# Moving a decay factor from the output of eight retention jobs into the turn of their q

## The chip, the cores and the metric

The kernel runs on one core of a Trainium2 chip. Its time is the device time of one execution in microseconds (us). Before the change three runs took 1150.2, 1152.78 and 1153.15 us, median 1152.78.

## The reference

Retention attention over q, k, v of shape (8 batches, 8 heads, 576 positions, 64), float32, is followed by a gated feed-forward block on 4608 tokens of width 512 (inner width 1536):

```python
gamma = 1.0 - 2.0 ** (-5.0 - np.arange(H))
Dmat  = np.where(rel >= 0, gamma[:, None, None] ** rel, 0.0)      # rel = i - j
attn  = ((q @ k.T) / np.sqrt(64) * Dmat) @ v                      # by batch and head
x     = attn.transpose(0, 2, 1, 3).reshape(4608, 512)
xn    = x / np.sqrt(mean(x * x) + 1e-6) * rms_g
out   = (silu(xn @ w_gate) * (xn @ w_val)) @ w_out
```

The three weight matrices come as 64-bit floats and are rounded to 32 bits in the kernel.

## The kernel before

A *job* is one batch and one pair of heads: 32 jobs, whose tiles hold two heads of 64 on 128 partitions. A *unit* is 384 tokens of the feed-forward block: 12 units. The instructions of each engine stand in the order in which the Python code writes them (a manual schedule), and each engine works through its own list in order.

A job works in chunks of L = 64 positions, nine in all. The decay gamma^(i-j) is split into a factor of the row and one of the column. Column factors gv scale v (`scale_v`, L255, ScalarE). Row factors, gamma^(i+L)/8 in the table gq, are applied to the result: `carried` (L362) multiplies it by gq when it copies it from PSUM into x (L390, VectorE). In between `scores` (L272) multiplies q and k within a chunk, `states` (L292) multiplies k and v, `weigh` (L305, VectorE) masks the scores, `sums` (L319, VectorE) adds up the states over chunks, `values` (L344) multiplies masked scores and v, and the products in `carried` add q times the summed states. A memset of one element, `tick`, on GpSimd (L359) stands between values and carried products.

`slot(j)` (L397) does values of job j-1, scores, states, masking and sums of job j, and the carried products of job j-1. The first eight jobs (j < 2*NHP, two batches) are loaded as they lie in memory by `load_first` (L145), and `turn(j)` (L216) turns their q and k on TensorE: for q, eight matrix products of a slice of q with the identity `ident` (L230); for k, four transposes (L224); for the last 64 rows, the tails, two transposes (L238). ScalarE copies the results into qT and kT (L235, L244). Later jobs are turned by VectorE in `prepare`, and use the tables gq and gx in `carried`.

`start()` (L846) writes out the beginning. Small tables are sent by `table(i, queue)`, chunk 0 of the weights by ScalarE's queue, the loads of the eight jobs by SP's queue. Then, for each of eight jobs: `slot(j)`, `turn(j + 1)`, adding up of squares, `scale_v`, the square of x of the job before (L432, ScalarE), steps of the weights' rounding (VectorE at L752 to L797, three Relu on ScalarE at L768), and for unit 0 `norm_1`, `diagonals` and `norm_2`. From L905 on the products of units 0 and 1 (`up_plain`, L564) follow, with the rounding of the other chunks beside them. Rows 8 and up of `w_up`, the tiles w_gate and w_val, hold data on its way at that time; columns 256 and up of rows 0 to 7 are not written until the second group of weight chunks.

Units 2 to 11 use seven block products instead of eight (`up` at L507, `across` at L629), with the later jobs in between. GpSimd makes the sums of weight blocks for that in `combine` (L811).

Of the kernel before, what the change touches and what calls it, by code (L numbers as in the profile page):

```python
# [22 lines left out]
def _decay_tables(H, D):  # L23

    pairs = _gamma(H).reshape(H // 2, 2).T
    rows = np.repeat(pairs, D, axis=0)
    pos = np.arange(L)
    p = np.concatenate([pos, pos])  # L30
    gq = rows[:, :, None] ** (pos + L) / np.sqrt(D)
    t = pairs.T[None] ** -p[:, None, None], rows**L, gq, np.roll(gq, D, axis=0)
    return [np.ascontiguousarray(x).astype(np.float32) for x in t]


# [6 lines left out]
def kernel(  # L42
# [64 lines left out]
    gx = const.tile([P, NHP, L], F32, name="gx")  # L107
    gv = const.tile([P, NHP, 2], F32, name="gv")
    gc = const.tile([P, NHP], F32, name="gc")
    tick = const.tile([1, 1], F32, name="tick")  # L110
    rms_g = const.tile([P, NHP], F32, name="rms_g")
    w_out = const.tile([P, NF, DM], F32, name="w_out")
# [87 lines left out]
    def load_kv(j):  # L200
# [12 lines left out]
            out=t, in_=v[b, 2 * hp : 2 * hp + 2, NFULL * P :].rearrange("e p d -> p e d")  # L213
        )

    def turn(j):  # L216

        d = st[j]
        last = bank(f"turn_{j}_t")
        for nm in "qk":  # L220
            ps = bank(f"turn_{j}_{nm}")
            for c in range(NFULL):
                if nm == "k":
                    nc.tensor.transpose(  # L224
                        out=ps[:, c * P : c * P + P],
                        in_=d["k"][:, c].rearrange("p e d -> p (e d)"), identity=ident,
                    )
                    continue
                for e in range(2):
                    nc.tensor.matmul(  # L230
                        ps[side(e), c::NFULL], lhsT=d["q"][:, e, c], rhs=ident,
                        start=True, stop=True,
                    )
            t = d[nm + "T"] = att.tile([P, S], F32, tag=nm + "T", name=f"{nm}T_{j}")
            nc.scalar.copy(out=t[:, : NFULL * P], in_=ps)  # L235
        for i, nm in enumerate("qk"):
            o = slice(i * TAIL, i * TAIL + TAIL)
            nc.tensor.transpose(  # L238
                out=last[:, o], in_=d[nm + "t"].rearrange("p e d -> p (e d)"),
                identity=ident[:TAIL, :TAIL],  # L240
            )
        for i, nm in enumerate("qk"):
            o = slice(i * TAIL, i * TAIL + TAIL)
            nc.scalar.copy(out=d[nm + "T"][:, NFULL * P :], in_=last[:, o])  # L244
# [117 lines left out]
    def carried(j):  # L362

        d = st[j]
        b, hp = jobs[j]
        av = d["av"]
        for c in range(1, NC):
            i, odd = divmod(c, 2)
            for e in range(2):
                mm = nc.tensor.matmul(  # L370
                    av[odd][column(j, odd, e), i * L : i * L + L], lhsT=d["sum"][side(e), c - 1],
                    rhs=d["qT"][side(e), c * L : c * L + L],
                    start=False, stop=(c >= NC - 2), skip_group_check=True,
                )
                if c == 1 and e == 0:
                    follow(mm, d["valued"])
        for c0, c1 in ((0, 2 * HU), (2 * HU, S)) if b % 2 == 0 else ((0, HU), (HU, S)):
            u, o = divmod(b * S + c0, U)
            if u not in x_of:
                x_of[u] = xp.tile([P, NHP, U], F32, tag="x", name=f"x_{u}")  # L380
            x = x_of[u][:, hp, o : o + c1 - c0].rearrange("p (c k) -> p c k", k=L)
            for first in (c0 // L, c0 // L + 1):
                i, odd = divmod(first, 2)
                n = -(-(c1 // L - first) // 2)
                moves = [(slice(0, P),) * 2]
                if column(j, odd, 0) != side(0):
                    moves = [(side(e), column(j, odd, e)) for e in range(2)]
                for to, at in moves:
                    g = (gq if to == at else gx)[at, hp].unsqueeze(1)
                    nc.vector.tensor_tensor(  # L390
                        out=x[to, first - c0 // L :: 2],
                        in0=av[odd][at, i * L : (i + n) * L].rearrange("p (c k) -> p c k", k=L),
                        in1=g.to_broadcast([at.stop - at.start, n, L]), op=ALU.mult,
                    )
        st[j] = {}
# [450 lines left out]
    def start():  # L846

        h_of[0] = ffn.tile([P, NF, U], F32, tag="h", name="h_0")
        tables = list(zip((causal, gv, gc, gq, gx), (_causal_table(), *_decay_tables(H, D))))

        def table(i, queue):
            t, values_ = tables[i]
            src = nc.inline_tensor(values_, name=t.tensor.name + "_table")
            queue.dma_start(out=t, in_=src.ap())

        make_identity(nc, ident)
        nc.scalar.activation(out=tick, in_=mhalf[:1], func=AF.Silu)
        nc.vector.memset(ones, 1.0)
        warm = bank("warm")
        for _ in range(6):  # L860
            nc.tensor.matmul(warm[:, :P], lhsT=ones, rhs=ones, start=True, stop=True)
        first_places.update(find_places())
        load_chunks(1)
        for i in (1, 0, 2):
            table(i, nc.scalar)
        weights(3)
        for j in range(2 * NHP):
            load_first(j, {0: range(2), 1: range(2, H), NHP: range(H)}.get(j))
            if j == 1:
                table(3, nc.sync)  # L870
            load_chunks((1, 1, 1, 1, 2, 2, 2, 3)[j], nc.sync)
        table(4, nc.sync)
        nc.sync.dma_start(out=rms_g, in_=moe_rms_g.rearrange("(c p) -> p c", p=P))
        load_chunks(4, nc.sync)
        turn(0)
        scale_v(0)
        act(3)
        squares = []
        for j in range(2 * NHP):
            slot(j)  # L880
            if j + 1 < 2 * NHP:
                turn(j + 1)
            if squares:
                gather(*squares.pop())
            for i in ((1,), (2,), (3,), (4, 5), (6,), (7,), (), ())[j]:
                scale_v(i)
            if j:
                u, c = divmod(j - 1, NHP)
                squares.append((u, c, square(u, c)))
            act(1)  # L890
            if j == 5:
                norm_1(0)
            elif j == 6:
                norm_2(0)
            weights((2, 0, 0, 1, 1, 1, 1, 0)[j])
            if j == 4:
                gather(*squares.pop())
            elif j == 5:
                diagonals(0)
            act(1)  # L900
        gather(*squares.pop())
        load_qk(2 * NHP)
        load_kv(2 * NHP)
        made = combine_out()
        for m, g in [(m, g) for g in range(NG) for m in range(2)]:  # L905
            for u in range(2):
                weights_to(4 * g + 2 * m + 1)
                for i, _ in enumerate(up_plain(u, m, g)):
                    if not (u or m or g):
                        if i == 0:  # L910
                            values(2 * NHP - 1)
                            carried(2 * NHP - 1)
                            gather(1, NHP - 1, square(1, NHP - 1))
                        elif i == 1:
                            norm_1(1)
                        elif i == 2:
                            diagonals(1)
                        elif i == 3:
                            norm_2(1)
                    weights(2)  # L920
                    act(1)
                    if u and m and g == NG - 1:
                        weights_to(len(chunks))
                        next(made, None)
                    if i == 1:
                        weights_to(4 * g + 2 * m + 2)
        for _ in made:
            pass
        for blk, t in first_blocks.items():
            keep(blk, t)  # L930
        rest = across(1)
        next(rest)
        following(2 * NHP - 1)
        for i, _ in enumerate(rest):
            if i == 1:
                norm_0(2)
            elif i == 3:
                norm_1(2)
                diagonals(2)
        rest = across(0)  # L940
        next(rest)
        combine(1)
        slot(8, rest=False)
        following(8)
        for i, _ in enumerate(rest):
            if i == 2:
                norm_2(2)
        combine(0)
        slot(9)
        following(9)  # L950
# [71 lines left out]
```

## Time and profile before

| | |
|---|---|
| median of three runs | 1152.78 us |
| the profiled execution | 1153.15 us, span 1151.4 us |
| TensorE (PE) busy | 1126.5 us, 98% of the span |
| VectorE (DVE) busy | 716.0 us, 62% |
| ScalarE (ACT) busy | 244.0 us, 21% |
| GpSimd (POOL) busy | 50.8 us, 4% |
| chain that ended last | PE 90%, DVE 3%, DMA 2% |

The profile is one execution. In its rows a line such as L390 is a line of the kernel before; a row of the timeline has the start in us from the span's start, the time in us, the engine, the line, the operation, the tile written and the tile read, the shape, the number of instructions merged, and in brackets the engine's idle time before it with what ended it. "ACTq" and "SPq" are the queues' own instructions, DMA issues among them. "issue" is time in which an engine waited for nothing that the profile shows. The granted clock is TensorE's, 1.00 being full speed.

### The profile page before, as it was taken

Reading aid. Unit: us, or ns where it says so; the run is one execution under the profiler, and the core shown is the slowest. Engines: PE = TensorE matmul, PEld = TensorE weight load, DVE = VectorE, ACT = ScalarE, POOL = GpSimd, SP = SyncE. Lnnn points to the kernel's source line nnn. Section 1 sums busy time; section 2 is a strip of 40 time slices with the busy share of each in tenths; the row PEclk is TensorE's granted clock in tenths of the full one; section 3 lists DMA queues with packets and bytes.
Section 4 is the critical chain, followed back from the end, with each engine's and each line's share of the span. In section 5 each row is a group of like instructions: output and inputs, shape, how many; then the busy total and the mean of one; then the engine's idle time right before and its main releaser. Section 6 shows DMA issues by size and latency. Waiting matters only on the chain.

```text
span 1151.4 us, 24802 instructions
## 1 busy us (share of the span) xinstructions
PE 1126.5 (98%) x10524; PEld 1053.4 (91%) x10524; DVE 716.0 (62%) x1420; ACT 244.0 (21%) x480; POOL 50.8 (4%) x74
## 2 busy tenths in 40 slices
PE   8799999989999999999999999999999999999998
PEld 6655557989999999999999999999999999999998
DVE  5788858675675675365766675465576566445352
ACT  5546542002201211211221120120220220120210
POOL 0000000570000000000000000000000000000000
PEclk8999999999999999999999999999999999999999
DMA  8764336335453565044345456306436503403304
GB/s 203 207 184 147 109 131 193 56 59 117 115 130 67 146 141 160 1 105 102 97 119 73 116 144 119 114 29 120 117 80 140 144 19 93 128 1 99 122 1 110
DMA packets 292943, 125.42 MB, mean 109 GB/s; under 512 B 270432, under 2 KB 275808, under 8 KB 292832
## 3 DMA queue, kind: packets, MB, share of 16 engines
q1 hardware_dynamic: 282688, 107.66, 38.1%
q10 hardware_dynamic: 10144, 16.16, 4.3%
q8 instruction: 83, 1.36, 0.5%
q14 instruction: 28, 0.23, 0.1%
HBM read 108.83 MB, written 14.94 MB: 108 GB/s over the span
## 4 chain that ended last, share of the span: by engine, by line
PE 90%; DVE 3%; DMA 2%; POOL 1%; ACT 1%; issue 1%; SPq 0%; DVEq 0%; POOLq 0%; ACTq 0%
PE x L507 14%; PE w L507 14%; PE z L507 13%; PE up L564 8%; PE xo L629 8%; PE wo L629 7%; PE zo L629 7%; PE y L507 7%; PE yo L629 4%; PE av L351 2%; PE av L370 2%; PE s L280 2%; POOL w_gate L811 1%; PE s L300 1%; DMA w_gate<-in_moe_w_out_dram 1%
## 5 line engine op out<-in xcount | busy, mean ns | idle before, releaser
L531 ACT COPY m<-x 128x384 f32<-128x384 f32 x60 | 28.8, 479 | 449.8 <-PE x L507 425.5
L629 PE MATMUL xo<-h,w_out 128*128 128x192 f32 x528 | 90.3, 328 | 0.0
L507 PE MATMUL w<-sums,w_val 128*128 128x192 f32 x480 | 88.6, 328 | 0.6 <-DVE c L514 0.3
L507 PE MATMUL x<-x,w_gate 128*128 128x192 f32 x480 | 89.0, 329 | 0.0
L507 PE MATMUL x<-x,w_val 128*128 128x192 f32 x480 | 88.8, 328 | 0.0
L507 PE MATMUL z<-x,w_gate 128*128 128x192 f32 x480 | 87.8, 326 | 0.0
L507 PE MATMUL w<-sums,w_gate 128*128 128x192 f32 x480 | 87.8, 326 | 0.0
L507 PE MATMUL z<-x,w_val 128*128 128x192 f32 x480 | 87.8, 326 | 0.0
L629 PEld LDWEIGHTS xo<-h,w_out 128*128 128x128 f32 x528 | 85.9, 190 | 0.6
L629 PE MATMUL wo<-h,w_out 128*128 128x192 f32 x504 | 85.3, 326 | 0.0
L629 PEld LDWEIGHTS wo<-h,w_out 128*128 128x128 f32 x504 | 82.5, 190 | 0.0
L514 DVE TENSOR_TENSOR u<-m,y 128x384 f32<-128x384 f32 x60 | 33.1, 552 | 79.2 <-PE y L507 79.1
L507 PEld LDWEIGHTS w<-sums,w_val 128*128 128x128 f32 x480 | 79.2, 190 | 2.9 <-DVE c L514 2.9
L507 PEld LDWEIGHTS x<-x,w_gate 128*128 128x128 f32 x480 | 79.6, 191 | 0.5
L507 PEld LDWEIGHTS z<-x,w_gate 128*128 128x128 f32 x480 | 79.8, 190 | 0.0
L507 PEld LDWEIGHTS x<-x,w_val 128*128 128x128 f32 x480 | 79.1, 190 | 0.6
L507 PEld LDWEIGHTS z<-x,w_val 128*128 128x128 f32 x480 | 79.6, 190 | 0.0
L507 PEld LDWEIGHTS w<-sums,w_gate 128*128 128x128 f32 x480 | 79.6, 190 | 0.0
L514 DVE TENSOR_TENSOR h<-u,w 128x384 f32<-128x384 f32 x60 | 33.0, 551 | 71.0 <-PE w L507 71.0
L526 ACT ACTIVATE h<-h 128x384 f32<-128x384 f32 x90 | 47.1, 523 | 88.6 <-DVE h L514 88.6
L564 PE MATMUL up<-x,w_gate 128*128 128x384 f32 x192 | 63.3, 488 | 0.9 <-DVE x L476 0.7
L564 PE MATMUL up<-x,w_val 128*128 128x384 f32 x192 | 62.7, 487 | 0.2 <-ACT w_val L572 0.2
(170 smaller groups left out, 1769.8 us busy)
## 6 DMA issues: line engine op xcount, KB each, us to landing
w_out<-w_blocks SPq DMA_DIRECT2D x70, 768.0 KB, 5.1
out_dram<-o SPq DMA_DIRECT2D x368, 24.0 KB, 1.6
qraw<-in_q_dram SPq DMA_DIRECT2D x96, 72.0 KB, 2.7
kraw<-in_k_dram SPq DMA_DIRECT2D x96, 72.0 KB, 2.8
k<-in_k_dram SPq DMA_DIRECT2D x48, 128.0 KB, 3.0
v<-in_v_dram SPq DMA_DIRECT2D x48, 128.0 KB, 2.9
w_out<-in_moe_w_gate_dram ACTq DMA_DIRECT2D x5, 1024.0 KB, 5.8
w_out<-in_moe_w_out_dram ACTq DMA_DIRECT2D x3, 1024.0 KB, 4.9
```

Of the source, the lines that this page charges most:

```text
L280: nc.tensor.matmul(s[side(odd), e, i * L : i * L + L], lhsT=d["kT"][side(e), c * L : c * L + L], rhs=d["qT"][side(e), c * L : c * L + L], ...
L300: nc.tensor.matmul(o[side(e)], lhsT=d["k"][side(odd), i, e], rhs=d["v"][side(odd), i, e], start=True, stop=True,)
L351: mm = nc.tensor.matmul(av[odd][column(j, odd, e), i * L : i * L + L], lhsT=d["v"][side(odd), i, e] if c < NC - 1 else d["vt"][:, e], rhs= ...
L370: mm = nc.tensor.matmul(av[odd][column(j, odd, e), i * L : i * L + L], lhsT=d["sum"][side(e), c - 1], rhs=d["qT"][side(e), c * L : c * L + L],
L507: nc.tensor.matmul(ps[:, i * HU : i * HU + HU], lhsT=w_up[m][:, 2 * blk + c, cut], rhs=t_of[u][blk][:, c], start=(start and i == c == 0), ...
L514: nc.vector.tensor_tensor(out=o, in0=a, in1=pairs_of(ps), op=ALU.add)
L526: nc.scalar.activation(out=o, in_=c, func=AF.Silu)
L531: nc.scalar.copy(out=s1, in_=pairs_of(x_))
L564: nc.tensor.matmul(ps[:, :U], lhsT=w_up[m][:, 4 * half + c, i * P : i * P + P], rhs=x_of[u][:, c], start=(c == 0), stop=(c == NHP - 1),)
L629: nc.tensor.matmul(ps[:, i * HU : i * HU + HU], lhsT=a[:, c, i * P : i * P + P], rhs=rhs[:, c], start=(start and i == c == 0), stop=False, ...
L811: nc.gpsimd.tensor_tensor(out=o, in0=a, in1=b, op=op)
```

## The change

The row factor gamma^(i+L)/8 of the first eight jobs goes into q when it is turned, instead of into the result. The right side of the products in `turn` is no longer the identity but a diagonal matrix of factors: by head, four of 128 x 128 and one of 64 x 64 for the tail. They lie in columns of w_gate and w_val that are free at that time. Eight heads have the same factors in both batches, so they are made once, as products of the identity and a new table `turned` (128 x 40): for job 0 on VectorE, for jobs 1 to 3 on GpSimd. The tail of q becomes two products instead of half of the transposes. x is then a plain copy from PSUM, made by ScalarE in place of VectorE's product. The table `turned` is sent first on ScalarE's queue, ahead of chunk 0; the table gq, now needed by job 8 first, is sent after the loads of the eight jobs instead of after job 1's.

The words that came with the change also name the norm of the third unit; the diff has no line on it.

```diff
@@ _decay_tables
+    at = np.stack([(4 * np.arange(P) + i) % L for i in range(4)] + [np.arange(P) % L], axis=1)
+    t += (_gamma(H)[None, :, None] ** (at[:, None, :] + L) / np.sqrt(D),)
@@ new functions
+    def factors(j, e):
+        h = 2 * jobs[j][1] + e
+        main = w_up[0][:, h, 2 * P : 6 * P].rearrange("p (i t) -> p i t", t=P)
+        return main, w_up[1][:TAIL, h, 4 * P : 4 * P + TAIL]
+
+    def make_factors(j, engine):
+        for e in range(2):
+            main, tail = factors(j, e)
+            g = turned[:, 2 * jobs[j][1] + e]
+            engine.tensor_tensor(
+                out=main, in0=ident.unsqueeze(1).to_broadcast([P, NFULL, P]),
+                in1=g[:, :NFULL].unsqueeze(2).to_broadcast([P, NFULL, P]), op=ALU.mult,
+            )
+            engine.tensor_tensor(
+                out=tail, in0=ident[:TAIL, :TAIL],
+                in1=g[:TAIL, NFULL:].to_broadcast([TAIL, TAIL]), op=ALU.mult,
+            )
@@ turn
-                        ps[side(e), c::NFULL], lhsT=d["q"][:, e, c], rhs=ident,
+                        ps[side(e), c::NFULL], lhsT=d["q"][:, e, c], rhs=factors(j, e)[0][:, c],
...
-        for i, nm in enumerate("qk"):
-            o = slice(i * TAIL, i * TAIL + TAIL)
-            nc.tensor.transpose(
-                out=last[:, o], in_=d[nm + "t"].rearrange("p e d -> p (e d)"),
-                identity=ident[:TAIL, :TAIL],
-            )
+        for e in range(2):
+            nc.tensor.matmul(
+                last[side(e), :TAIL], lhsT=d["qt"][:, e], rhs=factors(j, e)[1],
+                start=True, stop=True,
+            )
+        nc.tensor.transpose(
+            out=last[:, TAIL : 2 * TAIL], in_=d["kt"].rearrange("p e d -> p (e d)"),
+            identity=ident[:TAIL, :TAIL],
+        )
@@ carried
                 for to, at in moves:
+                    if j < 2 * NHP:
+                        nc.scalar.copy(
+                            out=x[to, first - c0 // L :: 2],
+                            in_=av[odd][at, i * L : (i + n) * L].rearrange("p (c k) -> p c k", k=L),
+                        )
+                        continue
                     g = (gq if to == at else gx)[at, hp].unsqueeze(1)
@@ start
+        table(5, nc.scalar)
         load_chunks(1)
         for i in (1, 0, 2):
             table(i, nc.scalar)
+        for j in range(NHP):
+            make_factors(j, nc.gpsimd if j else nc.vector)
         weights(3)
         for j in range(2 * NHP):
             load_first(j, {0: range(2), 1: range(2, H), NHP: range(H)}.get(j))
-            if j == 1:
-                table(3, nc.sync)
             load_chunks((1, 1, 1, 1, 2, 2, 2, 3)[j], nc.sync)
+        table(3, nc.sync)
         table(4, nc.sync)
```

More of the change, by code (lines that the diff above doesn't have):

```diff
@@ L109 @@
     gc = const.tile([P, NHP], F32, name="gc")
+    turned = const.tile([P, H, NFULL + 1], F32, name="turned")
     tick = const.tile([1, 1], F32, name="tick")
@@ L848, in start @@
         h_of[0] = ffn.tile([P, NF, U], F32, tag="h", name="h_0")
-        tables = list(zip((causal, gv, gc, gq, gx), (_causal_table(), *_decay_tables(H, D))))
+        tables = list(zip((causal, gv, gc, gq, gx, turned), (_causal_table(), *_decay_tables(H, D))))
         def table(i, queue):
```

## The prediction

> **What bounds the kernel now.** I began with TensorE's time by stage, since the edits lie in the first eight jobs. Columns: stage, its length, busy time of PE, PEld, DVE, ACT, POOL, granted clock, DMA share, GB/s.
>
> ```profile
> 0.00:75.00 75.00, 61.59 (x1356) 48.97 (x1356) 52.10 (x153) 37.98 (x87) 4.85 (x16) 0.93 0.80 200
> 75.00:180.00 105.00, 104.70 (x324) 61.55 (x325) 82.32 (x95) 59.40 (x70) 0.00 (x0) 1.00 0.38 128
> 10.00:20.00 10.00, 9.76 (x252) 8.54 (x253) 7.21 (x19) 7.38 (x17) 0.09 (x1) 0.74 0.96 217
> ```
>
> From 75 us on TensorE has no idle time that the change could reach (104.70 of 105.00). So the change is worth what it moves the products of the two first units, at 68.34 and 75.09 us. Next the timeline of the first job: what holds ScalarE and the clock there.
>
> ```profile
> 3.75 0.36 ACTq L854 DMA_DIRECT2D gv<-gv_table  x1
> 4.05 1.56 PE L230 MATMUL turn_q<-ident,h 128*64 128x128 f32 x16
> 6.63 0.69 DVE L752 TENSOR_SCALAR w_gate<-w_out 128x1024 uint32<-128x1024 uint32 x1 [5.50 <-DMA w_out<-in_moe_w_gate_dram]
> 7.90 0.33 ACTq L854 DMA_DIRECT2D causal<-causal_table  x1
> 8.02 0.69 PE L224 MATMUL turn_k<-ident,first_k 128*128 128x128 f32 x4 [2.41 <-DMA first_k<-in_k_dram]
> 8.76 0.59 ACT L235 COPY qT<-turn_q 128x512 f32<-128x512 f32 x1 [6.54 <-DMA gv<-gv_table]
> 9.93 0.54 ACT L260 ACTIVATE first_sums<-first_sums,gv 128x256 f32<-128x256 f32 x1
> ```
>
> ScalarE's queue issues gv, causal and gc, and its first copy comes after the last of them (8.28 + 0.44). From 9.93 to 15.25 ScalarE is the chain: four scalings, three Relu of 1.15, the next copies. Then the timelines of slots 6 and 7, for VectorE, and of the rounds of weights on GpSimd, for what two engines cost each other.
>
> ```profile
> 48.48 0.94 DVE L390 TENSOR_TENSOR x<-av,gq 128x128 f32<-128x128 f32 x4
> 56.11 2.19 DVE L476 SCALAR_TENSOR_TENSOR x<-x,rms_g,rb 128x384 f32<-128x384 f32 x4
> 62.36 0.28 DVE L329 SCALAR_TENSOR_TENSOR sum<-sum,gc,last 128x64 f32<-128x64 f32 x1
> 62.56 0.94 DVE L390 TENSOR_TENSOR x<-av,gq 128x128 f32<-128x128 f32 x4
> ```
>
> ```profile
> 210.06 1.32 DVE L641 TENSOR_TENSOR w_val<-w_val 128x1152 f32<-128x1152 f32 x1
> 218.62 2.35 DVE L641 TENSOR_TENSOR t<-h 128x1152 f32<-128x1152 f32 x1
> L811 POOL TENSOR_TENSOR w_val<-w_val x12: 1269/1274/2385, 215.8 to 233.6; 128x512 f32<-128x512 f32 x12
> ```
>
> The same subtraction took 1.32 us with GpSimd idle and 2.35 with GpSimd at work, and GpSimd's own 1.27 grew to 2.39 at worst.
>
> **The change, part by part** (times of the profiled execution, line numbers of before).
>
> *x on ScalarE.* VectorE loses 8 x 0.94 = 7.5 us. ScalarE gains four copies a job. A 512-column copy starts 0.58 after the one before it, a 64-column one 0.11, so 1.05 ns a column and 0.04 each; columns 192, 192, 128, 64 make 0.24 + 0.24 + 0.17 + 0.11 = 0.76 us a job. They stand ahead of the qT copy, which waits for turn_q anyway: 16 records, 1.09 us. That hides them; without it they cost 0.76 x 7 = 5.3. If they don't overlap (0.22 for 64 columns alone, so 1.22 together) 0.13 shows in each of seven slots, 0.9 in all. In slots 2 and 3 the second scaling of v ends last (27.72 + 0.51, the products of L300 at 28.35), so VectorE's relief is worth nothing there. In the slot of turn 6 the copies stand behind the Relu that ends at 46.98, so qT 6 starts near 47.75 instead of 46.89; but the six products of ms (48.09 to 48.85) come first on TensorE, and values start near 48.95 instead of 48.85. Price 0.1, ends 0 and 0.86.
>
> *VectorE's relief.* It lies between 45 and 66 us, where VectorE is nearly full. Without x at 48.48, r (49.35) can follow ms, which ends at 48.92, and GpSimd's power and the diagonals come 0.4 earlier. L476 starts when rb ends, and rb, by the waits in the built order, no longer waits for ScalarE's kT (55.16, idle 0.24 before). So the sums of job 7, which end at 62.64, end some 0.3 earlier if TensorE's pause of 1.01 at 49.65 (put down to "issue") remains, and 0.4 + 1.0 = 1.4 earlier if it goes. TensorE waited 0.55 for these sums. After them x of jobs 6 and 7 leaves VectorE, but the square of job 7 now waits for all four copies instead of two, 0.15 later. I take -0.8, the middle, ends -1.4 and -0.3.
>
> *Start.* The table turned goes out first on ScalarE's queue, so chunk 0 is issued about 0.45 later (0.43 an issue). The built order shows that DMAs share eight semaphores in turn, so each waits for the one eight before it. With one more in front, gv waits for k (7.90) where it waited for q (3.75), causal for chunk 0, gc for the tail of k. Causal, issued at 7.90, took 2.5 to land; gv then lands near 10.4 to 10.5, and the scalings that start at 9.93 wait: 0.5 us, with the Relu and the next job's copies queued behind. Ends 0.35 (the issue alone) and 1.1 (gc's 3.1 landing).
>
> Job 0's factors are four VectorE products, two of 512 columns at 0.69 (0.55 for 384 in L438, plus 128 x 1.04 ns) and two of 64 at about 0.2: 1.8 us. No row has the table's landing; q's 3.0 and gv's 5.0 bound it, I take q's, the issue nearest in time: 3.8. But GpSimd's twelve products are released by the same landing: six of 1.35 (three took 3.97 in a row) and six of about 0.25, 9.6 us. By the row of L641 a product loses about 1.0 to the other engine. The second half's factor, needed by turn_q's second product, then ends at 7.0 (VectorE first) or 8.35 (GpSimd first). turn_q takes 1.09, or 1.97 at half clock as at 12.20, turn_k 0.66 or 1.12. So turn_k ends between 8.8 and 11.4 instead of 8.71. In the first case ScalarE's copies set the scores (9.1 + 0.5 + 0.6 = 10.2), in the second turn_k does (11.4 + 0.6 + 0.1): 0.3 to 2.3 after 9.89. Rounding of chunk 0 (0.69, 0.69, 1.23) shifts from 6.63 to about 8.8, with a wait for GpSimd each, to 13.1 us; the masked scores began at 12.29. The two delays overlap. I take +1.2, ends +0.5 and +2.3: nearer to the low end, since the Relu from 11.2 covers part. GpSimd ends its list near 17.9 (3.8 + 9.6 + 4.4 of VectorE's turns); the first tick memset, which waited until 16.39, is queued behind it, and carried products (17.6 now, 18.8 then) wait for that tick.
>
> [...]
>
> *gq's table moved.* It passes the loads of jobs 2 to 7 on SP: 0.61 of issue and 128 KB less ahead of them. Only job 5's v was waited for (1.86 + 0.26), in a stretch where TensorE paused 2.33 for its own reasons. I take -0.2, ends -0.6 and 0. It then stands before gx, rms_g and one chunk, whose loads win as much before: nothing.
>
> *Turns of q, tails.* Same products with another right side. A tail is two products and a transpose: five records for two, some 0.02 us each (40 of L280 in 0.76), 0.5 in all, within the 0.24 us that values waited after each turn. Nothing, ends -0.3 and +0.5. TensorE's five pauses under "issue" (0.35, 1.07, 2.33, 1.01, 0.81) come at heavy DMA; the change hardly alters that. Nothing, ends -2 and +2.
>
> *The third unit's norm.* The change's words name it, no line of the diff touches it, and the built order has it in one place in both: nothing.
>
> **Sum.** +1.2 - 0.2 + 0.1 - 0.8 = +0.3 us. The ends without the pauses: 0.5 - 0.6 + 0 - 1.4 - 0.3 = -1.8 and 2.3 + 0 + 0.9 - 0.3 + 0.5 + 0.9 = +4.3. The profiled execution was 1153.15 us, of which the span is 1151.4; the median of the runs is 1152.78. On the median: 1153.1.
>
> **Rivals.** No difference beyond 0.3% (3.5 us, about what a measurement of this kernel can tell from no change) is the forecast: a late start given back by VectorE. 0.65.
>
> *Slower, by GpSimd's list.* Place: first tick and the factors of job 0. If the table lands like gv, after 5.0 us (at 5.9), GpSimd ends near 20.0 and VectorE's factor near 10.4; turn_q at half clock ends at 12.4, turn_k at 13.5, and after a copy of 0.6 the scores start near 14.2, 4.3 later than 9.89. It decides once the second factor is later than k's landing (7.9) by more than the 0.8 that the relief gives back. +4.3 - 0.8 + 0.1 = +3.6, 1156.4 us; more with copies that don't overlap. [...] Against: q landed in 3.0. 0.20.
>
> *Faster, by the relief.* The pause at 49.65 moves off the chain and relief is 1.4 us; the 2.33 pause at 35.87 and the half clock after it (turn_q 1.98 for 1.09, turn_k 1.12 for 0.66) go, because job 5's loads are earlier: 0.5 - 1.4 - 2.33 - 1.35 = -4.6, of which ScalarE's chain behind job 5's v (its last scaling starts at 37.97) gives back about 0.8. -3.8, 1149.0 us. For it: TensorE waited for sums of job 7. Against: the DMA queue stays full (share 1.04 in 30 to 40). 0.15.
>
> *ScalarE becomes the bound* lies inside the forecast: +0.9 at most.
>
> **Range.** From the faster case, 1149.0, to the slower one with the copies in part exposed, 1157.0; beyond either lies some 1 in 10.
>
> **What would show it.** Right: gv issued near 8 us, scores of job 0 starting between 10.2 and 12.2, L390's place taken by ScalarE copies of 0.76 to 1.22 us a job, values of job 7 before 62.56 plus the delay at the start, and TensorE without idle time after 75 us. Wrong: GpSimd's factors over 1.9 us each, a first tick that carried products wait for by over 1 us, copies of x that turn_q doesn't hide, or pauses under "issue" that differ by more than 2 us in all.

## The result, and the profile after

The changed kernel took 1158.82 us (median of four runs, 1157.52 to 1159.65) against 1152.61 us for the kernel before on the same chip: 6.2 us more, ratio 1.0057 with a 95% interval of 1.004 to 1.0074. Its profiled execution was 1159.65 us, span 1157.8. The kernel became slower, by 0.6%.

The stages first, in the columns of the prediction, and as a fourth one the later part that the prediction had called full.

```profile
0.00:75.00 75.00, 63.25 (x1372) 51.45 (x1373) 51.36 (x122) 42.10 (x117) 15.69 (x28) 0.93 0.80 200
75.00:180.00 105.00, 104.13 (x323) 60.90 (x322) 81.81 (x95) 57.86 (x66) 0.00 (x0) 1.00 0.39 129
10.00:20.00 10.00, 7.94 (x194) 6.67 (x198) 9.39 (x16) 7.49 (x18) 5.03 (x7) 1.00 0.92 208
620.00:960.00 340.00, 333.58 (x3478) 328.07 (x3477) 208.77 (x450) 57.91 (x130) 3.62 (x15) 1.00 0.40 98
```

The same late stretch of the kernel before:

```profile
620.00:960.00 340.00, 339.53 (x3515) 333.61 (x3515) 213.78 (x460) 58.82 (x131) 3.62 (x15) 1.00 0.42 100
```

Between 620 and 960 us, where no line of the diff is at work, TensorE is busy 333.58 us of 340 instead of 339.53. That is 5.95 us, about the whole loss. The waits of TensorE from 75 us on say what it waited for. Columns: waiting tile and line, what it waited for, us in total, times, longest.

```profile
PE av L397 <- issue: 4.6, 3, 1.7
PE av L397 <- POOL tick L386: 3.4, 2, 3.1
PE x L540 <- issue: 1.5, 1, 1.5
```

Before there was one such pause under "issue" after 75 us, 0.9 us long; now four make 6.1 us. One of them in the timeline of TensorE:

```profile
649.84 0.22 PE L397 MATMUL av<-qT,sum 64*64 64x64 f32 x1
649.85 0.22 PE L327 MATMUL s<-v,k 64*64 64x64 f32 x1
649.85 0.62 PE L397 MATMUL av<-qT,sum 64*64 64x64 f32 x24
652.06 0.34 PE L397 MATMUL av<-qT,sum 64*64 64x64 f32 x7 [1.59 <-issue]
```

Carried products stop in the middle of a row of equal products, and the profile shows no input that they wait for. I counted TensorE's records up to each such pause of 0.3 us or more: weight loads, products and its sequencer's own instructions, nearly all of them waits for semaphores (165 in the kernel before, 175 after the change), in order of start. In the kernel before they stand at records 706, 1218, 1475, 1986, 2498 and 5570; after the change at 1218, 1730, 12738, 13250, 16322 and 18114. Divided by 256 all of these leave 194 or 195; counted without the sequencer's, the remainders drift (184 at the first pause before, 152 at the last). So the pauses stand at fixed places in the instruction stream, a whole number of 256 records apart; a *block* below is 256 records from one such place on. The DMA table has a queue of kind "instruction" with 83 packets of 16 KB, and the records, 21213 before and 21271 after the change, are 82.9 and 83.1 blocks:

```profile
q8 instruction: 83, 1.36, 0.5%
```

With 256 records more, in the run with 64 products below, it has 84. So I read a packet as one block. In the 14 profiles of this study there are 69 such pauses after 12 us, and not one stands elsewhere. TensorE went on 1.23 to 1.71 us after the end of the block's packet; at none of the 1151 block starts that I could match did it go on earlier than 1.22 us behind a packet. The packet itself takes about 1 us (0.88 to 1.73 before and after the change). In the pauses it starts after TensorE has entered the block before: 1.15 to 4.3 us after in the first 75 us, where loads are dense (DMA share 0.80), and 0.5 to 3.6 us after later on. In the long products 256 records take some 20 us (20.3 is the median of all blocks before), and no late block follows such a stretch. In a slot, with its products of 64 x 64, a block is gone sooner: those ahead of the late ones took 2.1 to 4.0 us without the pause, and 2.75 to 6.0 us in the first 75 us.

The change adds 48 weight loads and products (10548 of each instead of 10524). A tail that was two transposes (two loads, two products) is now two matrix products and one transpose, and each of these matrix products leaves two loads and two products:

```profile
51.91 0.33 PE L261 MATMUL turn_t<-w_val 64*64 64x64 f32 x4
52.17 0.27 PE L265 MATMUL turn_t<-ident,w_val 64*128 64x64 f32 x1
```

That is six more a job, for eight jobs. With them come ten more waits of the sequencer, so that from slot 8 on every block begins some 58 records earlier in the work, and other work stands at the block starts. The expectations below count the 48 alone.

The start, as the timeline has it:

```profile
4.14 1.55 POOL L231 TENSOR_TENSOR w_gate<-ident,turned 128x512 f32<-128x512 f32 x1 [2.84 <-DMA turned<-turned_table]
5.69 0.68 DVE L231 TENSOR_TENSOR w_gate<-ident,turned 128x512 f32<-128x512 f32 x1
6.30 5.30 DVE L235 TENSOR_TENSOR w_val<-ident,turned 64x64 f32<-64x64 f32 x1
7.67 0.34 ACTq L887 DMA_DIRECT2D gv<-gv_table  x1
8.06 0.44 ACTq L887 DMA_DIRECT2D causal<-causal_table  x1
8.32 1.11 PE L248 MATMUL turn_k<-ident,first_k 128*128 128x128 f32 x4
9.03 0.59 ACT L259 COPY qT<-turn_q 128x512 f32<-128x512 f32 x1 [6.81 <-PE turn_q L254]
11.53 0.68 DVE L785 TENSOR_SCALAR w_gate<-w_out 128x1024 uint32<-128x1024 uint32 x1
11.65 0.47 PE L261 MATMUL turn_t<-w_val 64*64 64x64 f32 x2 [1.81 <-DVE w_val L235]
12.35 1.34 PE L307 MATMUL s<-qT,kT 64*64 64x64 f32 x40
```

VectorE's last factor, of 64 x 64, took 5.30 us: GpSimd ran eight products back to back meanwhile (6.49 to 11.51 us). The rounding of chunk 0 follows at 11.53 instead of 6.63 us, turn_t waits 1.81 us, and the scores of job 0 start at 12.35 instead of 9.89 us.

### The profile page after: what moved, and what is told of

Read it like the earlier page. It is cut to its first block, busy times and chain, and to the rows that moved or that the text cites. A ratio compares the mean times of both kernels' runs of the same rounds, so it can differ in the third digit from the quotient of the medians.

```text
span 1157.8 us, 24873 instructions
## 1 busy us (share of the span) xinstructions
PE 1129.5 (98%) x10548; PEld 1056.1 (91%) x10548; DVE 716.4 (62%) x1392; ACT 250.1 (22%) x512; POOL 61.6 (5%) x86
## 4 chain that ended last, share of the span: by engine, by line
PE 91%; DVE 3%; DMA 2%; POOL 2%; issue 1%; ACT 1%; DVEq 0%; POOLq 0%
PE x L540 14%; PE w L540 13%; PE z L540 13%; PE xo L662 8%; PE wo L662 8%; PE zo L662 8%; PE up L597 8%; PE y L540 7%; PE yo L662 4%; PE av L397 2%; PE av L378 2%; POOL w_gate L844 1%; PE s L307 1%; PE s L327 1%; DMA w_gate<-in_moe_w_out_dram 1%
## 5 line engine op out<-in xcount | busy, mean ns | idle before, releaser
L547 DVE TENSOR_TENSOR u<-m,y 128x384 f32<-128x384 f32 x60 | 33.1, 552 | 79.4 <-PE y L540 79.4
```

The costliest lines, as they stand in the source:

```text
L547: nc.vector.tensor_tensor(out=o, in0=a, in1=pairs_of(ps), op=ALU.add)
```

## Experiments

Three theories. P ("port" in the expectations; what the two engines share is not shown): GpSimd's factors starve VectorE at the start, 2.5 us that stay. B (blocks): the added records shift the blocks, and the pauses come from there. C (rival): the copies of x on ScalarE and the longer tails cost the time directly. Line numbers below are each kernel's own.

### The changed kernel again

No edit.

> The changed kernel unaltered, to see which of its pauses come back. Theory P (port): the 2.5 us by which the scores of job 0 start late (12.35 against 9.89 us) come again, and so do most of the 6 us. Theory B (blocks of instructions): TensorE's pauses under issue stand only at every 256th record (counts that leave 194 when divided by 256), and if the place in the work decides, the four late ones (652, 674, 843, 928 us; 6.1 us in all) come again at the same records; if the chance of the run decides, at others. About 1158.8 us by both.

Measured: 1159.38 us, ratio to before 1.0074 (1.0055 to 1.0093). Scores of job 0 at 12.5 us. The late pauses stand at the same four records, 12738, 13250, 16322 and 18114, with 1.83, 0.96, 2.31 and 1.45 us: the place in the work decides that they come, the run how long they are. In the first 75 us record 1218 came again (2.35), 1730 not, and 2243 was new (1.11): there the run decides more.

### One set of factors, GpSimd's products left out

```diff
-        h = 2 * jobs[j][1] + e
+        h = e
...
-        for j in range(NHP):
-            make_factors(j, nc.gpsimd if j else nc.vector)
+        make_factors(0, nc.vector)
```

> All first eight jobs use job 0's factors and GpSimd's twelve products are left out (the factors of heads 2 to 7 are wrong by that). Theory P: VectorE's fourth factor ends near 6.7 us instead of 11.6, the scores of job 0 start between 9.9 and 10.5, and the kernel comes out 2 to 3.6 us under the changed one: 1155.2 to 1156.8. Theory B alone: the start is shorter but the pauses take its place; within 1 us of 1158.8. Theory C (the copies of x on ScalarE and the longer tails cost the time): no difference, 1158.8.

The first eight jobs all use the factors of heads 0 and 1 here. Measured: 1158.69 us, 1.0060 (1.0047 to 1.0074). The starvation is gone: VectorE's second small factor takes 0.21 us and the scores start at 10.24.

```profile
5.51 0.21 DVE L235 TENSOR_TENSOR w_val<-ident,turned 64x64 f32<-64x64 f32 x1
7.33 0.69 DVE L785 TENSOR_SCALAR w_gate<-w_out 128x1024 uint32<-128x1024 uint32 x1 [1.61 <-DMA w_out<-in_moe_w_gate_dram]
10.24 1.35 PE L307 MATMUL s<-qT,kT 64*64 64x64 f32 x40 [0.57 <-ACT kT L259]
```

And the kernel is no faster. The block at record 1218 now came 4.06 us late (35.17 us, against 34.17 in the changed kernel). P, as the price of the change, falls. Why that block came later here is not shown.

### The same with q's tail transposed as before

```diff
-        for e in range(2):
-            nc.tensor.matmul(
-                last[side(e), :TAIL], lhsT=d["qt"][:, e], rhs=factors(j, e)[1],
-                start=True, stop=True,
-            )
-        nc.tensor.transpose(
-            out=last[:, TAIL : 2 * TAIL], in_=d["kt"].rearrange("p e d -> p (e d)"),
-            identity=ident[:TAIL, :TAIL],
-        )
+        for i, nm in enumerate("qk"):
+            o = slice(i * TAIL, i * TAIL + TAIL)
+            nc.tensor.transpose(
+                out=last[:, o], in_=d[nm + "t"].rearrange("p e d -> p (e d)"),
+                identity=ident[:TAIL, :TAIL],
+            )
```

> As the run with one set of factors, and besides q's tail is transposed with the identity as before the change (the last 64 positions lack the factor), so that TensorE has the same number of records as before the change. Theories P and B together: what is left is the table, VectorE's four products and the copies of x: 1152 to 1153.5, and pauses at the places in the work where the kernel before has them. Theory P without B: the same as the run with one set, within 0.7 us. Theory C: 1156 or more, since the copies stay.

The last 64 rows of q lack the factor in this kernel. Measured: 1151.69 us, 0.9997 (0.9987 to 1.0006), 7.0 us under the run above with x still copied by ScalarE. The one late pause is that of before, record 5571 (2.05 us); from 330 us on there is none of 0.3 us. This speaks for B and against C.

### Twelve products more in the kernel before

```diff
+        for _ in range(12):
+            nc.tensor.matmul(
+                warm[:64, :64], lhsT=ones[:64, :64], rhs=ones[:64, :64], start=True, stop=True
+            )
         first_places.update(find_places())
```

> The kernel before with 12 more products of 64 x 64 on ones behind the warm-up, in time in which TensorE waits for the first loads: 48 records more, as the change adds by the end of slot 7, so that each block of 256 records begins earlier in the work. Theory B: the pauses under issue move to other work, and the time changes by 1 to 3 us, likeliest up: 1154 to 1155.5. Theories P and C: 1152.6, within 0.7 us.

Measured: 1160.98 us, 1.0091 (1.0074 to 1.0107): no less than the change itself (1.0057 and 1.0074), from 12 idle products in time in which TensorE waits. The scores of job 0 start at 10.06 us. The waits after 330 us are those of the changed kernel, at the records 12738, 13250, 16322 and 18114, and besides one at 7874, where the changed kernel, whose blocks begin ten records earlier in the work, has none:

```profile
PE av L370 <- issue: 3.8, 3, 1.6
PE y L507 <- issue: 2.0, 1, 2.0
PE x L507 <- issue: 0.4, 1, 0.4
```

This kernel has no line of the change in it, so B alone can make a loss of this size. I had sized it at 1 to 3 us.

### Twelve and 64 products in the wait at 250 us

```diff
             states(j)
+        if j == 9:
+            for _ in range(12):
+                nc.tensor.matmul(
+                    st[j]["last"][:64, 64:128], lhsT=ones[64:, :64], rhs=ones[64:, :64],
+                    start=True, stop=True,
+                )
```

> The kernel before with 12 more products of 64 x 64 on ones between the scores of job 9 and the carried products of job 8, where TensorE waits 3.15 us for the tick on GpSimd (249.5 to 252.7 us): 48 records more from there on, nothing changed before. Theory B: the first 250 us stay as before, the pause at 297 us goes, and pauses come near 402, 652, 674, 843 and 928 us, as in the kernel with 12 more at the start: 3.5 to 6 us more, 1156 to 1158. Theories P and C: nothing, 1152.2 within 0.7.

> The same with 64 products, which are 256 records, one whole block (some 2.8 us inside the wait of 3.15): from there on each block begins at the same work as before the change. Theory B: the same time as before, 1152.2 within 0.7, with the one late pause near 297 us. If more records as such cost time (more to fetch), more than the run with 12: over 1158.

Measured with 12: 1155.38 us, 1.0035 (1.0023 to 1.0047), a little under what I expected; pauses of 1.18, 0.98, 0.38, 0.94 and 1.96 us at 398, 648, 670, 838 and 924 us, the expected five. With 64: 1154.88 us, 1.0025 (1.0014 to 1.0036), not the time of before. Its trace has no late pause but one of 1.06 us at 300.32, as expected of a whole block. But the 64 products took 7.39 us instead of 2.8, and the carried products came 4 us later for it:

```profile
249.43 7.39 PE L408 MATMUL last<-ones 64*64 64x64 f32 x124
256.62 0.27 PE L370 MATMUL av<-qT,sum 64*64 64x64 f32 x1
```

All 64 stood in the same quarter of the array and took 0.115 us each; the products of values, which I had priced them by (16 in 0.69 us), take turns over four quarters. The miss is the price of the filling, not the blocks: the profile is 2.4 us behind that of the kernel before at 260 us and 2.8 at the end.

### The changed kernel with 52 products in that wait, in one place and spread

```diff
+            for n in range(52):
+                row, col = divmod(n, 2)
+                r = side(row % 2)
+                o = st[j]["last"][side(col), 64:128] if row % 2 else st[j]["s"][side(col), 2, 448:]
+                nc.tensor.matmul(o, lhsT=ones[r, :64], rhs=ones[r, :64], start=True, stop=True)
```

In one place (written as above for 64):

> The changed kernel with 52 products (208 records) in that wait: with the change's own 48 they make one whole block, so that from 256 us on the blocks begin at the same work as before the change. Theory B: the late pauses (652, 674, 843, 928 us) go, the one near 297 us comes back: 1153 to 1155 instead of 1159, what is left being the 2 to 3.5 us of the first 75 us less what the tick wait gives back. Theories P and C: 1158.8, no change.

Spread over four quarters:

> The changed kernel with the 52 products in the wait of 3.15 us once more, now taking turns over the four quarters of the array and two banks, so that they run side by side: 52 x 43 ns = 2.2 us by the row of the first products of values (16 in 0.69 us), inside the wait, where the 64 in one place took 7.39 us. Theory B: no late pause but the one near 300 us, nothing lost at 250 us: from 330 us on like the kernel before with the start of the changed one, 1154 to 1156, 3 to 5 us under the changed one. If the late pauses are not due to where blocks begin: 1158.8.

With the sequencer's ten waits the fill makes 266 records, ten past a whole block. In one place: 1158.87 us, 1.0062 (1.0047 to 1.0077), no change in the time. The late pauses went (one of 0.71 us at 573 us was left), but the filling took 52 x 0.115 = 6.0 us, 2.9 more than the wait, and the pause near 300 us came back (1.18 us); in the medians nothing of the gain is left. Spread: 1154.07 us, 1.0020 (1.0011 to 1.0029), with the whole change still in it. After 330 us TensorE waited for

```profile
PE x L546 <- issue: 0.4, 1, 0.4
PE av L397 <- POOL tick L386: 0.3, 1, 0.3
```

and the late stretch is as full as before the change (339.53 there):

```profile
620.00:960.00 340.00, 339.51 (x3516) 333.59 (x3515) 213.81 (x460) 59.25 (x132) 3.60 (x15) 1.00 0.41 100
```

The 52 products took 1.7 us (251.4 to 253.2). So 208 idle records take some 5 us off the changed kernel: 1.0057 to 1.0074 in its two measurements, 1.0020 here, intervals apart.

### The changed kernel with plain tails, all factors made

The edit of the tails above alone.

> The changed kernel with all its factors made, GpSimd's twelve products too, but with q's tail transposed with the identity (the last 64 positions lack the factor), so that TensorE has the records of before: the price of theory P alone, beside the run with one set and plain tails (1151.7). Theory P: rounding of chunk 0 is starved until 11.5 us as in the changed kernel, and the up products of the second group start 1 to 2.5 us later than there: 1152.5 to 1154.2. Theory B alone: 1151.7, within 0.8.

Measured: 1152.08 us, 1.0007 (0.9994 to 1.002). VectorE is starved as in the changed kernel, and the time is that of before within 0.2%:

```profile
6.49 5.30 DVE L235 TENSOR_TENSOR w_val<-ident,turned 64x64 f32<-64x64 f32 x1
11.72 0.68 DVE L782 TENSOR_SCALAR w_gate<-w_out 128x1024 uint32<-128x1024 uint32 x1
```

With this run the four make a square. This last run stands beside another measurement of the kernel before (1151.52 us) than the other three (1152.22), so the ratios are surer than the medians. By the ratios the records cost 0.63% without GpSimd's products (1.0060 against 0.9997) and 0.67% with them (1.0074 against 1.0007), 7.3 and 7.7 us. GpSimd's products cost 0.10% without the records and 0.14% with them, 1.2 and 1.6 us (0.4 and 0.7 by the medians), with intervals that overlap. The second unit's up products start at 73.7 us here and at 72.2 in the run with one set, 1.5 us apart. So P is not told from nothing, nor from 1 to 1.5 us; it is not the 6 us. In this run turn_t no longer needs the starved factor, so this is P without that wait.

### Another way with the records of before

q is multiplied in place, then turned with the identity, its tail by a transpose as before; x is copied by ScalarE. Job 0's products are VectorE's, ahead of the rounding; the others are GpSimd's, ahead of the slot before their turn, for jobs 2 and 5 behind it.

```diff
+    def scale_q(j, engine, between=0):
+        d = st[j]
+        h = slice(2 * jobs[j][1], 2 * jobs[j][1] + 2)
+        g = turned[:, h, :NFULL].unsqueeze(3).to_broadcast([P, 2, NFULL, D])
+        engine.tensor_tensor(out=d["q"], in0=d["q"], in1=g, op=ALU.mult)
+        weights(between)
+        g = turned[:TAIL, h, NFULL:].to_broadcast([TAIL, 2, D])
+        engine.tensor_tensor(out=d["qt"], in0=d["qt"], in1=g, op=ALU.mult)
...
-                        ps[side(e), c::NFULL], lhsT=d["q"][:, e, c], rhs=factors(j, e)[0][:, c],
+                        ps[side(e), c::NFULL], lhsT=d["q"][:, e, c], rhs=ident,
```

> Another way to the same end, with as many TensorE records as before the change: q itself is multiplied in place by the factors of its rows (job 0 by VectorE, the others by GpSimd, one product of 128 x 512 and one of 64 x 128 a job, spread over the slots), then turned with the identity and tail transposes as before; x copied by ScalarE. Theory B with C false: no late pauses beyond the one near 297 us, and the first 75 us as in the run with one set and plain tails: 1150.5 to 1153. If the copies of x or GpSimd's products cost time on their own: 1154 or more, with late sums or copies in slots 5 to 7.

Measured: 1152.71 us, 1.0013 (1.0001 to 1.0026), 1149.84 to 1157.06. No late pause after 330 us. Moving x to ScalarE and the factors into q is worth nothing by itself, within 0.3%.

### The tick of job 8 on ScalarE

```diff
-        d["valued"] = nc.gpsimd.memset(tick, 0.0)
+        if j == 8:
+            d["valued"] = nc.scalar.copy(out=tick, in_=mhalf[:1])
+        else:
+            d["valued"] = nc.gpsimd.memset(tick, 0.0)
```

In the kernel before, and in the one with q scaled in place:

> The kernel before with the tick of job 8 alone made by ScalarE, which idles there from 237 to 255 us, instead of GpSimd, whose tick stands behind twelve subtractions: the wait of 3.15 us goes, and with it the half clock after it (254.2 to 257.6 in the trace, worth 1.7): 1147.5 to 1149.5. If the products that follow need GpSimd's subtractions at once, the wait only moves: 1151.5 or more.

> q scaled in place, x copied by ScalarE, TensorE's records as before, and the tick of job 8 on ScalarE: the gain of that tick on top of 1152.7: 1148 to 1150, beside the kernel before with the same tick. If it comes out under that one by over 1 us, the idea of the change is worth something without its records; if not, it is worth nothing.

Measured: 1150.46 us, 0.9994 (0.9979 to 1.0008), and 1149.16 us, 0.9982 (0.997 to 0.9994). In both the wait of 3.15 us is gone. In the first, a block met the slot that now came earlier:

```profile
267.90 0.56 PE L373 MATMUL av<-qT,sum 64*64 64x64 f32 x22
270.45 0.38 PE L373 MATMUL av<-qT,sum 64*64 64x64 f32 x9 [1.98 <-issue]
```

with half clock from 271.7 to 275.1 us behind it (granted clock 0.98 over 240 to 330 us, 1.00 in the second kernel), which gave most of the wait back. In the second the same block was not late (one pause, 1.28 us at 291.55). So the last kernel is the one that beats both, by 0.2% against before. Whether its q in place has a share in that is unclear: 1.3 us between the two medians, with intervals that overlap.

### All profiles together

The two shifts are of the block starts against the kernel before, in records, the sequencer's waits among them, near 60 us and from 256 us on; 256 is again none. A block's own shift can be up to four less, since the order of starts varies. "Second unit" is the start of its up products (75.09 us before), "late" the sum of pauses of 0.3 us or more after 330 us.

| kernel | shift | second unit, us | late, us | ratio |
|---|---|---|---|---|
| before | 0, 0 | 75.1 | 0 | 1 |
| changed | 57, 58 | 78.7 | 6.06 | 1.0057 |
| changed, again | 57, 58 | 77.3 | 6.55 | 1.0074 |
| one set | 57, 58 | 77.9 | 5.33 | 1.0060 |
| one set, plain tails | 4, 5 | 72.2 | 0 | 0.9997 |
| before, 12 more at the start | 48, 48 | 76.7 | 6.17 | 1.0091 |
| before, 12 in the wait | 0, 48 | 73.0 | 5.44 | 1.0035 |
| before, 64 in the wait | 0, 256 | 75.3 | 0 | 1.0025 |
| changed, 52 in one place | 57, 266 | 78.2 | 0.71 | 1.0062 |
| q scaled | 6, 7 | 72.7 | 0 | 1.0013 |
| changed, plain tails | 4, 5 | 73.7 | 0 | 1.0007 |
| changed, 52 spread | 57, 266 | 77.7 | 0.35 | 1.0020 |
| before, tick on ScalarE | 0, 2 | 72.5 | 0 | 0.9994 |
| q scaled, tick | 6, 9 | 73.8 | 0 | 0.9982 |

Every kernel with a late shift of 48 or 58 has the late pauses; those within ten records of none (0 to 9, 256, 266) have 0.71 us at most. From 335 us to the end, by the starts of the same products in two profiles, the five kernels with the late pauses lost 4.8 to 7.8 us against the kernel before, the other eight between -0.4 and +0.2.

Every kernel with an early shift of 48 or 57 starts the second unit at 76.7 or later, every other at 75.3 or earlier. That margin is thin: the four kernels that are the kernel before up to 240 us started it at 75.1, 73.0, 75.3 and 72.5 us.

## Why the prediction was wrong

**The step that failed** is the term for TensorE's pauses under "issue": "Nothing, ends -2 and +2", since "the change hardly alters that". I took them for a matter of dense DMA; five in a row at distances of 256 and 512 records would have told that they are blocks, and six more records a job, with the waits that they bring, that the blocks move. With it fell the sentence on which the sum stood, "From 75 us on TensorE has no idle time that the change could reach": by the table the change put 5.3 to 6.6 us of pauses there.

**How the 6.2 us come about.** In the one pair of profiles: +3.6 at the second unit; -2.5 between 243 and 326 us, where the pause of 0.92 us and the half clock after the tick's wait (254.2 to 257.6, 1.7 us) are not in the changed kernel's profile; +5.5 from there on. That makes 6.6, where the spans differ by 6.4. By medians the late blocks are about 5 us (spread filling). The early shift is 1.5 to 2 (that run against the one with plain tails, 1.0020 and 1.0007, 1154.07 and 1152.08 us), with intervals that overlap. How the early part splits into pauses, half clock and waits behind them is open: it differs from run to run, and there is one profile of each kernel.

**Start, +1.2 with ends +0.5 and +2.3.** The queue's order was right: gv was issued at 7.67, causal at 8.06, qT copied at 9.03. The scores were 2.46 us later, just over the high end. The step that failed is that whole instructions alternate between VectorE and GpSimd, an assumption of mine on which the 7.0 and 8.35 stand; no run shows it as a rule. VectorE's first three products fit it (0.69, 1.06 and 0.68 us); the fourth, put at about 0.2, took 5.30, while GpSimd ran eight. What makes one product last through eight is not shown. Whether +1.2 was right as a price is open: the square gives 0.4 to 1.6 us, with intervals that overlap. One reading of the kernel before was wrong too: from 9.89 to 15.23 us its recorded chain runs on TensorE (turn_q for job 1 at half clock, 1.90 us from 12.27), where the prediction has ScalarE as the chain from 9.93 to 15.25.

**The slower rival** came near the time (1156.4) by luck, since its mechanism is another. Its condition, VectorE's second factor later than k's landing, did not hold: that factor ended at 6.37, and the starved one was the tail's. GpSimd's list ended at 14.9, ahead of the first tick (18.83). Without GpSimd's list the kernel took 1158.69, with the list but without the records 1152.08.

**Copies of x** were right: 0.83 us for four, hidden behind turn_q in most slots; where they showed (the tail of turn 6 in the run with one set and plain tails) it was 0.80, inside the bound of 0.9.

**VectorE's relief, -0.8** was not seen, nor excluded. The sums of job 7 ended at 65.99 us, 3.35 after those of before, which is more than the start's delay. The three runs with x on ScalarE and the records of before, at 0.9997, 1.0007 and 1.0013, leave room for about a microsecond either way.

**Tails: "Nothing".** As time on TensorE right (0.53 us for a tail), as a count wrong: five records were meant, there are ten with the weight loads, for four.

**What would show it wrong** named pauses under "issue" that differ by more than 2 us in all. In the first 75 us they sum to 5.57 before and 4.65 after; over the span they differ by 4.2. So this sign came true over the span, by the late blocks.

## What to carry to other kernels

Where TensorE is full, look where its pauses under "issue" stand in the count of its instructions, its sequencer's waits among them, before calling them noise. Here they lay a whole number of 256 apart, and an edit that added records, however cheap, moved the blocks through all the work that followed; its price was that of the new places (8.8 us for 12 idle products). Test it by adding idle instructions to the kernel before, and weigh an edit with its count made up to a whole block, spread over the array's quarters in a wait that exists (52 products took 1.7 us so, 6.0 in one quarter).

## What the runs showed of the hardware

The packet of TensorE's next block started about when the block before it began (0.3 us after that in the median of the profiles, 4.3 at most), and TensorE entered a block no earlier than 1.22 us after its packet's end. The sequencer's waits count among the 256 (remainders of 194 or 195 with them, 184 to 152 without). After 75 us the late blocks stand behind blocks of 2.1 to 4.0 us, none behind the 20 us of the long products; not every short block had a late one behind it (one of 1.88 us, at its end at 317.96 us before, had none). Twelve idle 64 x 64 products put the kernel before 8.8 us behind.

VectorE's product of 64 x 64, 0.21 us alone, took 5.30 us beside GpSimd's products in two kernels (the changed one, and with plain tails). Products of 64 x 64 in one quarter of the array took 0.115 us each, those that take turns over four quarters 0.043 us (16 of values in 0.69 us) and 0.033 us (the 52 of the filling in 1.7).

In the profiles of before and after TensorE has six pauses of 1.98 to 3.15 us. In or within 1.6 us after five of them the granted clock fell to 0.50, for 3.4 or 6.8 us (8.5 to 15.3, 39.2 to 42.6 and 254.2 to 257.6 us before; 33.1 to 40.0 and 46.8 to 50.2 after); behind the sixth, of 3.12 us at 256.16 after, it stayed at 1.00, as behind the four late blocks after the change (1.26 to 1.74 us). By an estimate, half of 3.4 us, a late block followed by half clock, as the one of 1.98 us with the tick on ScalarE, can so cost its pause and 1.7 us more.
